# A spectral filter and a maxout MLP on one core: x of six batches loaded as bf16 for a dense first transform, in place of fp32 loads that are folded for a half-size one

## The chip, the cores and the metric

The kernel runs on 1 core of one Trainium2 chip. The metric is the device time of that core in microseconds (us), for one execution of the whole program. Lower is better.

## The reference

The reference is a real Fourier transform along the sequence, a product with a filter, the inverse transform, and then a small MLP with a maxout in the middle, on every token:

```
x: (8, 3072, 256) fp32;  filt_r, filt_i: (1537, 256);  w1, w2: (256, 1024);  w_out: (1024, 256)
X = rfft(x, axis=1);  Y = X * (filt_r + 1j * filt_i);  y = irfft(Y, n=3072, axis=1)
h1 = y @ w1;  h2 = y @ w2;  g = maximum(h1, h2);  out = g @ w_out        # (24576, 256) fp32
```

## The kernel before, in words

All of it is matmuls on TensorE (PE). The sequence of 3072 is split into 128 x 24. For each of the 8 batches the stages are:

- **f1**: the transform over the 128, as a matmul with the table C1. x stands in SBUF with 128 sequence rows as partitions and `n`, one of 24, beside the 256 features. The result is written to DRAM (tile `ad`) and read back in another order (`bt`, by `f1_read`).
- **f2** (`gen_f2`): eight steps `g` per batch. Each makes the transform over the 24 (`px`, matmuls with the table U, in quadrants of PE), multiplies by the filter on VectorE (`pq`, two instructions of 120x1024), and makes the inverse transform over the 24 (`pz`, matmuls with VP and VQ), evacuates it on ScalarE (`zt`) and writes it to DRAM (`zd`). A step's `pz` part is issued one step after its `px` part. `z_read` reads the result back (`zr`).
- **s4**: the inverse transform over the 128 (`py`, with G1), for one of 6 token blocks of a batch (512 tokens each).
- **moe_h** and **moe_o**: the MLP for one token block `tt`, in 8 steps `j`. The maximum is made as relu(y (w1 - w2)) and an additive term y (w2 w_out). `moe_h` (line 595) makes one of 8 hidden tiles, with a relu on ScalarE (line 600) or, for some, on VectorE (line 598). `moe_o` (lines 615 and 620) makes the output tiles of the block before; every fourth step VectorE copies a half block into `ot` (line 622), and at `j == 7` GpSimd's queue (POOL) stores `ot` to DRAM (line 627). There are two `ot` buffers.

The first batch goes through an opening of its own (`first_s1` to `first_t2`), with tables made by sines on ScalarE and small POOL and VectorE instructions. After about 47.7 us the main loop starts: `for tt in range(49)`, in it `for j in range(8)`; the step number is `8 * tt + j`. Each step issues `moe_h(tt, j)`, `moe_o(tt - 1, j)`, then whatever a hand-written plan has put on that step, and then, at `j` of 4 (or 6), the next `s4`. The plan (`plan_x`, `plan_f2`, `plan`) is what places the transform of the following batches between the MLP of the present one. The schedule is manual: every engine and every queue runs its instructions in the order of issue.

Three things matter for what follows.

First, how x of batches 2 to 7 is loaded. `load_p` (line 395) issues two DMAs on the SyncE queue (SP) for each of 6 groups `c` of four `n`. They bring fp32 rows p and p + 64 side by side into `xf`, with the two halves in opposite order in the upper 64 partitions. Five steps later `fold_x` (line 402) makes their sums and differences on GpSimd as bf16 (`xd`), with two instructions. These stand in the same in-order queue as the stores of `ot` at line 627.

Second, `f1_half` (line 410), called within six of the eight steps of `gen_f2(b)` for batch b + 1. With the sums and differences, the 128-row transform is two of 64 rows each. It takes four 64x64 quadrant matmuls with 512 columns per group, into two PSUM buffers `pa`, two ScalarE evacuations (line 413), and one write of `ad`. The columns of C1 are permuted for that, even before odd, by two POOL copies in the opening (line 639).

Third, PSUM: `ps` is a ring of 6 buffers, which `ph`, `px`, `pa`, `pz` and `py` share in the order of issue; `po` has two of its own.

Batch 1's x is loaded as bf16 by POOL DMAs that cast (`load_x`, line 101) and goes through the dense `f1` (line 379 and after), with C1 as 128x128 weights.

`f1_read` (line 423) reads `ad` in 8 DMAs on SP: two halves, two blocks, and even and odd apart.

Of the kernel before, what the change touches and what calls it, by code (L numbers as in the profile page):

```python
# [8 lines left out]
FP32 = mybir.dt.float32  # L9
BF16 = mybir.dt.bfloat16  # L10
AF = mybir.ActivationFunctionType
OP = mybir.AluOpType

B = 8
N = 3072
D = 256
HID = 1024
N1 = 128
N2 = 24
# [6 lines left out]
QUADS = ((0, 0), (1, 1), (0, 1), (1, 0))  # L26
# [3 lines left out]
def kernel(  # L30
# [25 lines left out]
    nc = tc.nc  # L56
    V, S, G, TE = nc.vector, nc.scalar, nc.gpsimd, nc.tensor

    const = ctx.enter_context(tc.tile_pool(name="const", bufs=1))
    C1 = const.tile([128, 128], BF16)  # L60
# [8 lines left out]
    I128 = const.tile([128, 128], BF16)  # L69

    dram = ctx.enter_context(tc.tile_pool(name="dram", bufs=2, space=bass.MemoryType.DRAM))
    xpool = ctx.enter_context(tc.tile_pool(name="xpool", bufs=7))
    apool = ctx.enter_context(tc.tile_pool(name="apool", bufs=5))
    bpool = ctx.enter_context(tc.tile_pool(name="bpool", bufs=2))
    pqpool = ctx.enter_context(tc.tile_pool(name="pqpool", bufs=6))
    zpool = ctx.enter_context(tc.tile_pool(name="zpool", bufs=2))
    zrpool = ctx.enter_context(tc.tile_pool(name="zrpool", bufs=2))
    late = ctx.enter_context(tc.tile_pool(name="late", bufs=1))
    w2b = late.tile([128, 2, HID], BF16, tag="l1", name="w2b")
    w2T = late.tile([128, 8, D], BF16, tag="l2", name="w2T")  # L80
    setup = ExitStack()
    ps = None
    init = setup.enter_context(tc.tile_pool(name="init", bufs=1))
# [12 lines left out]
    xb = {}  # L96
# [107 lines left out]
    load_f(1)  # L204

    Ct = init.tile([128, 128], BF16)
    Cz = init.tile([128, 128], BF16)

    def table_c():
        V.memset(kc[:, :, 1, 0:1], 32.0)  # L210
        V.memset(kc[:, 1, 0, 0:1], 64.0)
        p128 = init.tile([128, 1], FP32)
        V.tensor_scalar(p128, pid, 1.0 / 128.0, None, OP.mult)
        uc = init.tile([128, 2, 2, T], FP32)
        rc = init.tile([128, 2, 2, T], FP32)
        V.tensor_scalar(uc[:, 0], kc[:, 0], p128, 0.25, OP.mult, OP.add)
        V.tensor_scalar(uc[:, 1], kc[:, 1], p128, 0.5, OP.mult, OP.add)
        V.tensor_scalar(uc[:, 1, 0, 0:1], kc[:, 1, 0, 0:1], p128, 0.25, OP.mult, OP.add)
        V.tensor_scalar(rc, uc, RND, RND, OP.add, OP.subtract)
        V.tensor_tensor(uc, uc, rc, OP.subtract)  # L220
        for a in range(2):
            for b in range(2):
                S.activation(Ct.rearrange("p (b a h c u) -> p a b c h u", b=2, a=2, h=4, c=2)[:, a, b],
                             uc[:, a, b].rearrange("p (c h u) -> p c h u", c=2, h=4), AF.Sin, bias=zero, scale=TWO_PI)
        Cv = Cz.rearrange("p (h c u b a) -> p a b c h u", h=4, c=2, b=2, a=2)
        for a in range(2):
            for b in range(2):
                S.activation(Cv[:, a, b], uc[:, a, b].rearrange("p (c h u) -> p c h u", c=2, h=4),
                             AF.Sin, bias=zero, scale=TWO_PI)
# [86 lines left out]

    def table_g():
        pg = p2.tile([128, 128], BF16, tag="px", name="pg", bufs=4)
        TE.transpose(pg, Cz, I128)
        S.activation(G1, pg, AF.Copy)  # L320

    def tables_q(h, E):
# [42 lines left out]
    bt = {}  # L365
    zr = {}

    ad = {}
# [12 lines left out]
        if c % 2 == 1:  # L381
            nc.sync.dma_start(out=ad[b][:, 2 * c - 2:2 * c + 2], in_=at)

    big = {}

    def load_p(b, c):
        if c == 0:
            big[b] = late.tile([128, 3, 2, 2 * D], FP32, tag="l0", name="xf")
        if c < 3:
            xb[b, c] = big[b][:, c]  # L390
        else:
            xb[b, c] = late.tile([128, 2, 2 * D], FP32, tag="l%d" % (c - 2), name="xf")
        for m in range(2):
            o = x.offset + (b * N + 4 * c + 2 * m + 64 * N2 * m) * D
            nc.sync.dma_start(out=xb[b, c][64 * m:64 * m + 64],
                              in_=bass.AP(x.tensor, o, [[N2 * D, 64], [(1 - 2 * m) * 64 * N2 * D, 2], [1, 2 * D]]))

    def fold_x(b, c):
        xf = xb[b, c]
        xb[b, c] = xpool.tile([128, 2, 2 * D], BF16, tag="xb", name="xd")  # L400
        for i, op in enumerate((OP.add, OP.subtract)):
            G.tensor_tensor(xb[b, c][:, i], xf[:, 0], xf[:, 1], op)  # L402

    def f1_half(b, c):
        if c == 0:
            ad[b] = dram.tile([128, N2, D], BF16, tag="ad", name="ad")
        at = apool.tile([128, 4, D], BF16, tag="at", name="at")
        pa = [ps.tile([128, 2, D], FP32, tag="ps", name="pa") for _ in range(2)]
        for m, i in QUADS:
            TE.matmul(pa[m][64 * i:64 * i + 64], C1[64 * m:64 * m + 64, 64 * i:64 * i + 64],  # L410
                      xb[b, c][64 * m:64 * m + 64, i], start=True, stop=True)
        for m in range(2):
            S.activation(at[:, 2 * m:2 * m + 2], pa[m], AF.Copy)  # L413
        nc.sync.dma_start(out=ad[b][:, 4 * c:4 * c + 4], in_=at)

    def f1_read(b):
        bt[b] = bpool.tile([128, T, D], BF16, tag="bt", name="bt")
        src = ad[b].rearrange("(e t b a) n d -> b (a n) e t d", e=2, b=2, a=2)
        for h in (1, 0):
            for blk in range(2):  # L420
                for e in range(2):
                    t0 = 16 * e + 8 * h
                    nc.sync.dma_start(out=bt[b][64 * blk:64 * blk + 48, t0:t0 + 8], in_=src[blk][:, e, 8 * h:8 * h + 8])  # L423


    def z_read(b, h):
# [5 lines left out]
    def gen_f2(b):  # L432
# [25 lines left out]
                zt = None  # L458

        made = []  # L460
        for j, g in enumerate((4, 5, 6, 7, 2, 3, 1, 0)):
            px = [ps.tile([128, 2, D], FP32, tag="ps", name="px") for _ in range(2)]
            for i in range(2):
                for k, c in QUADS:
                    t_ = 16 * i + 4 * (g // 2) + 2 * c + g % 2
                    TE.matmul(px[k][64 * c:64 * c + 64, i], U[64 * k:64 * k + 48, 4 * g + 2 * i + c],  # L466
                              bt_[64 * k:64 * k + 48, t_], start=True, stop=True)
            pq = []
            for k in range(2):
                pq.append(pqpool.tile([128, 2, 2, D], BF16, tag="pq", name="pq"))  # L470
                V.tensor_tensor(pq[k][0:FROWS],  # L471
                                px[k][0:FROWS].rearrange("p (o i) d -> p o i d", o=1).to_broadcast([FROWS, 2, 2, D]),
                                F[0:FROWS, :, k, 2 * g:2 * g + 2], OP.mult)
            if b + 1 < B and j in (0, 1, 3, 4, 6, 7):
                f1_half(b + 1, (0, 1, 3, 4, 6, 7).index(j))
            pend.append((g, pq))
            if len(pend) > 1:
                s3(*pend.pop(0))
            yield
# [153 lines left out]
    def drain(g):  # L633
        for _ in g:
            pass

    table_c()
    for e in range(2):
        G.tensor_copy(C1.rearrange("p (e x u w) -> p e x u w", e=2, x=8, u=2)[:, e],
                      Cz.rearrange("p (x u e w) -> p e x u w", x=8, u=2, e=2)[:, e])  # L640
    Zt = late.tile([128, 2, 128, N2], BF16, tag="l0", name="Zt")
    At = init.tile([128, 4, 64, T], BF16, name="At")
    zeros(At[:, :, 48:64].rearrange("p h m t -> p h (m t)"), [4, 512])
    zeros(U.rearrange("p t (q x) -> p (t q) x", q=2)[:, :, 24:32], [64, 8])
# [66 lines left out]
    ps = ctx.enter_context(tc.tile_pool(name="ps", bufs=6, space=bass.MemoryType.PSUM))  # L711
# [10 lines left out]
    def plan(step, fn, *a):  # L722
        todo.setdefault(step, []).append((fn, a))

    def plan_x(n, steps):
        for c, s_ in enumerate(steps):
            plan(s_, load_p, n, c)
            plan(s_ + 5, fold_x, n, c)

    def plan_f2(n, steps, z1, z0):  # L730
        g = []

        def go():
            if not g:
                g.append(gen_f2(n))
            next(g[0], None)

        for s_ in steps:
            plan(s_, go)
        plan(z1, z_read, n, 1)  # L740
        plan(z0, z_read, n, 0)

    def spaced(first, gap, count):
        return [first + int(gap * i) for i in range(count)]
# [4 lines left out]
        plan(int(0.6 * (c - 1)), f1, 1, c, (S, V)[c % 2])  # L749
    plan(6, f1_read, 1)  # L750
    plan_f2(1, spaced(17, 1.9, 9), 28, 34)
    plan_x(2, (5, 7, 8, 10, 11, 13))
    plan(36, f1_read, 2)
    plan_x(3, spaced(32, 3.5, 6))
    plan_f2(2, spaced(60, 2.5, 9), 74, 81)
    plan(83, f1_read, 3)
    plan_x(4, spaced(76, 3.5, 6))
    plan_f2(3, spaced(104, 3, 9), 121, 129)
    plan(130, f1_read, 4)
    plan_x(5, spaced(122, 3.5, 6))  # L760
    plan_f2(4, spaced(150, 3.3, 9), 168, 178)
    plan(179, f1_read, 5)
    for n in range(5, B):
        o = 48 * (n - 5)
        if n + 1 < B:
            plan_x(n + 1, spaced(168 + o, 3.5, 6))
            plan(227 + o, f1_read, n + 1)
        plan_f2(n, spaced(197 + o, 3.4, 9), 216 + o, 226 + o)

    def in_f2(step):  # L770
# [2 lines left out]
    for tt in range(6 * B + 1):  # L773
        b, i = divmod(tt, 6)
# [40 lines left out]
```

## Time and profile before

| what | value |
|---|---|
| median of 2 runs | 582.9 us (581.5 and 584.31) |
| the profiled execution: its own time | 581.5 us |
| its span, first to last instruction | 579.7 us |
| mean granted TensorE clock | 0.962 |
| ScalarE relus of line 600 | 308 of 602 ns, 181.6 us |
| main MLP matmuls, line 620 | 1536 of 128x256, 234.5 us |
| folds on GpSimd, line 402 | 72 of 1264 ns, 89.3 us |
| fp32 loads of x on SP, line 395 | 72 of 256 KB |
| bf16 loads of x on POOL, line 101 | 12, 10.1 us from issue to landing in the median |
| stores of `ot` on POOL, line 627 | 47 of 512 KB, 4.4 us to landing in the median |
| SP's queue: packets' share of 16 DMA engines over the span | 49.6% |
| POOL's queue: the same | 17.9% |

How to read the profile: engines are PE (TensorE matmul), PEld (TensorE weight load, which overlaps PE), DVE (VectorE), ACT (ScalarE), POOL (GpSimd) and SP (SyncE, which only issues DMAs here). A line of the slices cuts the span into 40 equal parts, a digit giving tenths of it busy; PEclk is the granted clock, in tenths of full speed. A line of waits names the engine, the group that waited and its line in the kernel, then after `<-` what released it, then microseconds in total, times, and the longest. A line of the timeline gives start, duration, engine, line, operation, tiles and shapes, with the idle time before it and its releaser in brackets. A line of windows gives the window, its length, busy microseconds (and instructions) of PE, PEld, DVE, ACT and POOL, the granted clock, the DMA engines' busy share, and GB/s.

### The profile page before, as it was taken

To read this page: it belongs to the slowest core of one execution; us is meant where nothing else is said; L and a number is where in the kernel's file an instruction comes from. 1 tells how busy PE (TensorE), PEld (TensorE's weight loads), DVE (VectorE), ACT (ScalarE), POOL (GpSimd) and SP (SyncE) were. 2 spreads that over 40 slices of the span, in tenths; PEclk is the share of its full clock that TensorE was granted. 3 is DMA by queue.
4 is the path that set the end of the run, shared out by engine and by line. 5 is a ranking of instruction groups with operands and counts; after the bars stand their busy time and mean duration, and the time that the engine had idled before them with its cause. 6 is when DMAs were issued, how large, how long until landed. Compare 5 with 4: busy or idle time off the path is not lost.

```text
span 579.7 us, 12530 instructions
## 1 busy us (share of the span) xinstructions
PE 520.9 (90%) x5206; PEld 352.9 (61%) x5284; DVE 322.5 (56%) x437; ACT 337.2 (58%) x597; POOL 147.9 (26%) x168
## 2 busy tenths in 40 slices
PE   8898859995999969995999996999789999999997
PEld 3556536663566646673566763676456766677775
DVE  8887437431773446542775346745377368734442
ACT  7777538643686546853566563755456556655452
POOL 6681163126004070232405240051400000000000
PEclk9999979998799989998999997999979999999999
DMA  8982995898368954989449983789535873451102
GB/s 150 275 142 87 166 259 154 233 197 198 137 177 226 211 177 128 265 164 209 142 137 286 204 176 122 202 234 210 173 101 156 166 171 93 119 155 73 72 39 109
DMA packets 74093, 97.03 MB, mean 167 GB/s; under 512 B 5106, under 2 KB 49780, under 8 KB 73044
## 3 DMA queue, kind: packets, MB, share of 16 engines
q1 hardware_dynamic: 63012, 63.72, 49.6%
q0 software_dynamic: 11024, 32.51, 17.9%
q8 instruction: 41, 0.67, 0.5%
q14 instruction: 16, 0.13, 0.1%
HBM read 54.79 MB, written 47.19 MB: 176 GB/s over the span
## 4 chain that ended last, share of the span: by engine, by line
PE 62%; DMA 18%; ACT 5%; DVE 5%; SPq 4%; issue 3%; POOL 2%; POOLq 0%; DVEq 0%; ACTq 0%
PE po L620 22%; PE ph L595 20%; DMA xf<-in_x_dram 6%; DMA out_dram<-ot 5%; PE po L615 5%; SPq L423 3%; PE pz L447 3%; ACT at L413 3%; PE px L466 3%; DMA zd<-zt 2%; PE py L579 2%; POOL xd L402 2%; DVE pq L471 2%; DMA bt<-ad 2%; PE pa L410 2%
## 5 line engine op out<-in xcount | busy, mean ns | idle before, releaser
L600 ACT ACTIVATE gt<-ph 128x512 bf16<-128x512 f32 x308 | 181.6, 602 | 131.9 <-PE ph L595 131.3
L620 PE MATMUL po<-Wo,gt 128*128 128x256 bf16 x1536 | 234.5, 277 | 4.0 <-issue 0.7
L620 PEld LDWEIGHTS <-gt 128*128 128x128 bf16 x1536 | 152.6, 99 | 61.1 <-issue 3.3
L622 DVE COPY ot<-po 128x512 f32<-128x512 f32 x96 | 66.3, 690 | 156.2 <-PE po L620 106.2
L471 DVE TENSOR_TENSOR pq<-px,F 120x1024 bf16<-120x1024 f32 x112 | 131.7, 1219 | 30.6 <-PE px L466 29.7
L402 POOL TENSOR_TENSOR xd<-xf 128x512 bf16<-128x512 f32 x72 | 89.3, 1264 | 141.9 <-DMA xf<-in_x_dram 102.3
L627 POOL DMA_DIRECT2D out_dram<-ot x47 | 25.7, 548 | 271.8 <-DVE ot L622 271.8
L595 PEld LDWEIGHTS <-Wd 128*128 128x128 bf16 x768 | 71.5, 99 | 28.5 <-issue 19.8
L451 ACT ACTIVATE zt<-pz 112x512 bf16<-112x512 f32 x112 | 60.9, 600 | 26.1 <-PE pz L447 24.9
L413 ACT ACTIVATE at<-pa 128x512 bf16<-128x512 f32 x72 | 39.1, 595 | 57.8 <-PE pa L410 57.8
L598 DVE TENSOR_SCALAR gt<-ph 128x512 bf16<-128x512 f32 x76 | 52.2, 687 | 34.6 <-PE ph L595 23.8
L410 PE MATMUL pa<-xd,C 64*64 64x512 bf16 x144 | 17.5, 405 | 28.1 <-DVE pq L471 15.2
L447 PE MATMUL pz<-pq,VP 56*64 56x256 bf16 x448 | 31.7, 283 | 7.0 <-DVE pq L471 4.9
L579 PE MATMUL py<-G,zr 128*128 128x128 bf16 x384 | 29.9, 219 | 1.8 <-ACT at L413 1.0
L447 PE MATMUL pz<-pq,VQ 56*64 56x256 bf16 x448 | 30.7, 281 | 0.0
L579 PEld LDWEIGHTS <-zr 128*128 128x128 bf16 x384 | 25.3, 98 | 5.1 <-issue 3.3
L466 PE MATMUL px<-bt,U 48*64 48x256 bf16 x448 | 24.2, 281 | 1.0 <-DMA bt<-ad 1.0
L410 PEld LDWEIGHTS <-C 64*64 64x64 bf16 x144 | 5.0, 109 | 30.6 <-DVE pq L471 16.6
L447 PEld LDWEIGHTS <-VP 56*64 56x64 bf16 x448 | 15.6, 109 | 11.6 <-issue 6.8
L466 PEld LDWEIGHTS <-U 48*64 48x64 bf16 x448 | 8.6, 104 | 13.5 <-issue 13.2
L447 PEld LDWEIGHTS <-VQ 56*64 56x64 bf16 x448 | 14.7, 111 | 1.8
L529 DVE TENSOR_TENSOR pq<-px,F 120x1024 bf16<-120x1024 f32 x11 | 13.2, 1220 | 2.4 <-issue 1.1
(388 smaller groups left out, 604.6 us busy)
## 6 DMA issues: line engine op xcount, KB each, us to landing
out_dram<-ot POOLq DMA_DIRECT2D x47, 512.0 KB, 4.4
xf<-in_x_dram SPq DMA_DIRECT2D x72, 256.0 KB
ad<-at SPq DMA_DIRECT2D x42, 256.0 KB
bt<-ad SPq DMA_DIRECT2D x56, 192.0 KB
zd<-zt SPq DMA_DIRECT2D x56, 192.0 KB
zr<-zd SPq DMA_DIRECT2D x14, 768.0 KB
xb<-in_x_dram POOLq DMA_DIRECT2D x12, 256.0 KB, 10.1
wf<-in_moe_w_dram POOLq DMA_DIRECT2D x2, 1024.0 KB, 10.3
```

The costliest lines, as they stand in the source:

```text
L402: G.tensor_tensor(xb[b, c][:, i], xf[:, 0], xf[:, 1], op)
L413: S.activation(at[:, 2 * m:2 * m + 2], pa[m], AF.Copy)
L447: TE.matmul(pz[c][64 * k:64 * k + 64, i], W[64 * c:64 * c + 56, 2 * g + i, k], pq[k][64 * c:64 * c + 56, ri, i], start=(ri == 0), stop=(ri ...
L451: S.activation(zt[0:ROWS, c, o:o + 2], pz[c][0:ROWS], AF.Copy)
L466: TE.matmul(px[k][64 * c:64 * c + 64, i], U[64 * k:64 * k + 48, 4 * g + 2 * i + c], bt_[64 * k:64 * k + 48, t_], start=True, stop=True)
L471: V.tensor_tensor(pq[k][0:FROWS], px[k][0:FROWS].rearrange("p (o i) d -> p o i d", o=1).to_broadcast([FROWS, 2, 2, D]), F[0:FROWS, :, k, 2 ...
L579: TE.matmul(py[:, n], zr[b][:, 4 * i + n, 128 * dc:128 * dc + 128], G1, start=True, stop=True)
L595: TE.matmul(ph, Wd[:, dc, 128 * j:128 * j + 128], y_[:, dc].rearrange("p a b -> p (a b)"), start=(dc == 0), stop=(dc == 1))
L598: V.tensor_scalar(gt[tt][:, j], ph, 0.0, None, OP.max)
L600: S.activation(gt[tt][:, j], ph, AF.Relu)
L620: TE.matmul(p_, g_[:, jj, 128 * n:128 * n + 128], Wo[:, jj], start=False, stop=(jj == 7))
L622: V.tensor_copy(ot[tt][:, n - 1:n + 1], po[tt])
```

## The change

`load_p`, `fold_x` and `f1_half` go. x of batches 2 to 7 is loaded by `load_x` as bf16 with a cast on POOL's queue, 6 DMAs per batch, as batch 1's is. The dense `f1` then runs for all of these batches, one 128x512 matmul and one ScalarE evacuation for two of the 24 `n`, each on a plan step of its own and not within `gen_f2`. `C1` is written by the sines at once, in the order that was `Cz`'s, without the two copies. `f1_read` reads `ad` with 4 DMAs of twice the size. `xpool` has 8 buffers in place of 7, and the tiles in `late` no longer share memory with `xf`. The order of `t_` in `gen_f2` follows the new order of `ad`. The plan is another: loads 4 steps apart, 12 calls of `f1` 1 to 1.9 steps apart after them, `f1_read` one or two steps after the last, and `gen_f2` where it was, but for batch 4, which moves by one step. The opening is otherwise the same.

```diff
-    xpool = ctx.enter_context(tc.tile_pool(name="xpool", bufs=7))
+    xpool = ctx.enter_context(tc.tile_pool(name="xpool", bufs=8))
...
-        Cv = Cz.rearrange("p (h c u b a) -> p a b c h u", h=4, c=2, b=2, a=2)
+        Cv = C1.rearrange("p (h c u b a) -> p a b c h u", h=4, c=2, b=2, a=2)
...
-    def load_p(b, c):
...
-        for m in range(2):
-            o = x.offset + (b * N + 4 * c + 2 * m + 64 * N2 * m) * D
-            nc.sync.dma_start(out=xb[b, c][64 * m:64 * m + 64],
-                              in_=bass.AP(x.tensor, o, [[N2 * D, 64], [(1 - 2 * m) * 64 * N2 * D, 2], [1, 2 * D]]))
-
-    def fold_x(b, c):
-        xf = xb[b, c]
-        xb[b, c] = xpool.tile([128, 2, 2 * D], BF16, tag="xb", name="xd")
-        for i, op in enumerate((OP.add, OP.subtract)):
-            G.tensor_tensor(xb[b, c][:, i], xf[:, 0], xf[:, 1], op)
-
-    def f1_half(b, c):
...
-        pa = [ps.tile([128, 2, D], FP32, tag="ps", name="pa") for _ in range(2)]
-        for m, i in QUADS:
-            TE.matmul(pa[m][64 * i:64 * i + 64], C1[64 * m:64 * m + 64, 64 * i:64 * i + 64],
-                      xb[b, c][64 * m:64 * m + 64, i], start=True, stop=True)
-        for m in range(2):
-            S.activation(at[:, 2 * m:2 * m + 2], pa[m], AF.Copy)
-        nc.sync.dma_start(out=ad[b][:, 4 * c:4 * c + 4], in_=at)
-
     def f1_read(b):
         bt[b] = bpool.tile([128, T, D], BF16, tag="bt", name="bt")
-        src = ad[b].rearrange("(e t b a) n d -> b (a n) e t d", e=2, b=2, a=2)
+        src = ad[b].rearrange("(t b a) n d -> b (a n) t d", b=2, a=2)
         for h in (1, 0):
             for blk in range(2):
-                for e in range(2):
-                    t0 = 16 * e + 8 * h
-                    nc.sync.dma_start(out=bt[b][64 * blk:64 * blk + 48, t0:t0 + 8], in_=src[blk][:, e, 8 * h:8 * h + 8])
+                nc.sync.dma_start(out=bt[b][64 * blk:64 * blk + 48, 16 * h:16 * h + 16],
+                                  in_=src[blk][:, 16 * h:16 * h + 16])
...
-            if b + 1 < B and j in (0, 1, 3, 4, 6, 7):
-                f1_half(b + 1, (0, 1, 3, 4, 6, 7).index(j))
...
     def plan_x(n, steps):
         for c, s_ in enumerate(steps):
-            plan(s_, load_p, n, c)
-            plan(s_ + 5, fold_x, n, c)
+            plan(s_, load_x, n, c)
+
+    def plan_f1(n, steps, read):
+        for c, s_ in enumerate(steps):
+            plan(s_, f1, n, c)
+        plan(read, f1_read, n)
...
-    plan_x(2, (5, 7, 8, 10, 11, 13))
-    plan(36, f1_read, 2)
-    plan_x(3, spaced(32, 3.5, 6))
+    plan_x(2, spaced(8, 4, 6))
+    plan_f1(2, spaced(34, 1, 12), 46)
     plan_f2(2, spaced(60, 2.5, 9), 74, 81)
-    plan(83, f1_read, 3)
-    plan_x(4, spaced(76, 3.5, 6))
+    plan_x(3, spaced(44, 4, 6))
+    plan_f1(3, spaced(70, 1.5, 12), 88)
     plan_f2(3, spaced(104, 3, 9), 121, 129)
-    plan(130, f1_read, 4)
-    plan_x(5, spaced(122, 3.5, 6))
-    plan_f2(4, spaced(150, 3.3, 9), 168, 178)
-    plan(179, f1_read, 5)
+    plan_x(4, spaced(90, 4, 6))
+    plan_f1(4, spaced(112, 1.8, 12), 132)
+    plan_f2(4, spaced(151, 3.3, 9), 169, 179)
     for n in range(5, B):
         o = 48 * (n - 5)
-        if n + 1 < B:
-            plan_x(n + 1, spaced(168 + o, 3.5, 6))
-            plan(227 + o, f1_read, n + 1)
+        plan_x(n, spaced(138 + o, 4, 6))
+        plan_f1(n, spaced(158 + o, 1.9, 12), 180 + o)
         plan_f2(n, spaced(197 + o, 3.4, 9), 216 + o, 226 + o)
```

More of the change, by code (lines that the diff above doesn't have):

```diff
@@ L78 @@
     late = ctx.enter_context(tc.tile_pool(name="late", bufs=1))
-    w2b = late.tile([128, 2, HID], BF16, tag="l1", name="w2b")
-    w2T = late.tile([128, 8, D], BF16, tag="l2", name="w2T")
+    w2b = late.tile([128, 2, HID], BF16)
+    w2T = late.tile([128, 8, D], BF16)
     setup = ExitStack()
@@ L206 @@
     Ct = init.tile([128, 128], BF16)
-    Cz = init.tile([128, 128], BF16)
     def table_c():
@@ L318, in table_g @@
         pg = p2.tile([128, 128], BF16, tag="px", name="pg", bufs=4)
-        TE.transpose(pg, Cz, I128)
+        TE.transpose(pg, C1, I128)
         S.activation(G1, pg, AF.Copy)
@@ L382, in f1 @@
             nc.sync.dma_start(out=ad[b][:, 2 * c - 2:2 * c + 2], in_=at)
-    big = {}
-    def load_p(b, c):
[L387 to L392, printed above, removed]
-        for m in range(2):
-            o = x.offset + (b * N + 4 * c + 2 * m + 64 * N2 * m) * D
-            nc.sync.dma_start(out=xb[b, c][64 * m:64 * m + 64],
-                              in_=bass.AP(x.tensor, o, [[N2 * D, 64], [(1 - 2 * m) * 64 * N2 * D, 2], [1, 2 * D]]))
-    def fold_x(b, c):
-        xf = xb[b, c]
-        xb[b, c] = xpool.tile([128, 2, 2 * D], BF16, tag="xb", name="xd")
-        for i, op in enumerate((OP.add, OP.subtract)):
-            G.tensor_tensor(xb[b, c][:, i], xf[:, 0], xf[:, 1], op)
-    def f1_half(b, c):
-        if c == 0:
-            ad[b] = dram.tile([128, N2, D], BF16, tag="ad", name="ad")
-        at = apool.tile([128, 4, D], BF16, tag="at", name="at")
-        pa = [ps.tile([128, 2, D], FP32, tag="ps", name="pa") for _ in range(2)]
-        for m, i in QUADS:
-            TE.matmul(pa[m][64 * i:64 * i + 64], C1[64 * m:64 * m + 64, 64 * i:64 * i + 64],
-                      xb[b, c][64 * m:64 * m + 64, i], start=True, stop=True)
-        for m in range(2):
-            S.activation(at[:, 2 * m:2 * m + 2], pa[m], AF.Copy)
-        nc.sync.dma_start(out=ad[b][:, 4 * c:4 * c + 4], in_=at)
     def f1_read(b):
         bt[b] = bpool.tile([128, T, D], BF16, tag="bt", name="bt")
-        src = ad[b].rearrange("(e t b a) n d -> b (a n) e t d", e=2, b=2, a=2)
+        src = ad[b].rearrange("(t b a) n d -> b (a n) t d", b=2, a=2)
         for h in (1, 0):
             for blk in range(2):
-                for e in range(2):
-                    t0 = 16 * e + 8 * h
-                    nc.sync.dma_start(out=bt[b][64 * blk:64 * blk + 48, t0:t0 + 8], in_=src[blk][:, e, 8 * h:8 * h + 8])
+                nc.sync.dma_start(out=bt[b][64 * blk:64 * blk + 48, 16 * h:16 * h + 16],
+                                  in_=src[blk][:, 16 * h:16 * h + 16])
     def z_read(b, h):
@@ L460, in gen_f2 @@
         made = []
-        for j, g in enumerate((4, 5, 6, 7, 2, 3, 1, 0)):
+        for g in (4, 5, 6, 7, 2, 3, 1, 0):
             px = [ps.tile([128, 2, D], FP32, tag="ps", name="px") for _ in range(2)]
@@ L464, in gen_f2 @@
                 for k, c in QUADS:
-                    t_ = 16 * i + 4 * (g // 2) + 2 * c + g % 2
+                    t_ = 8 * (g // 2) + 4 * c + 2 * (g % 2) + i
                     TE.matmul(px[k][64 * c:64 * c + 64, i], U[64 * k:64 * k + 48, 4 * g + 2 * i + c],
@@ L637 @@
     table_c()
[L638 to L641, printed above, removed]
+    Zt = late.tile([128, 2, 128, N2], BF16, name="Zt")
     At = init.tile([128, 4, 64, T], BF16, name="At")
```

## The prediction

> **What bounds the kernel now.** I read the busy table and the slices first, then the waits, then one stall in order of time, then the same stretch of work batch by batch.
>
> ```profile
> PE 520.9 (90%) x5206; PEld 352.9 (61%) x5284; DVE 322.5 (56%) x437; ACT 337.2 (58%) x597; POOL 147.9 (26%) x168
> PE   8898859995999969995999996999789999999997
> PEclk9999979998799989998999997999979999999999
> ```
>
> TensorE (PE) is the bound at 90%, and no other engine is near. Seven slices fall below 9 after the opening, and near each the granted clock falls too. The waits say who holds PE there:
>
> ```profile
> POOL out_dram L627 <- DVE ot L622: 271.8, 33, 14.1
> POOL xd L402 <- DMA xf<-in_x_dram: 102.3, 12, 17.4
> DVE ot L622 <- DMA out_dram<-ot: 49.7, 6, 11.1
> PE pa L410 <- DVE pq L471: 15.2, 5, 6.4
> PE pa L410 <- POOL xd L402: 7.0, 2, 6.4
> PE pa L410 <- DVE y__4127 L584: 5.9, 1, 5.9
> PE pz L447 <- DVE pq L471: 4.9, 2, 4.2
> ```
>
> PE's last four rows are 33.0 us in ten waits. The third row has six waits of some 8 us, one to a batch, and the second is long enough to be behind them. In order of time, one of the six, from the timeline of DVE and that of all engines (start, duration, engine, line; the wait before it in brackets):
>
> ```profile
> 120.45 0.69 DVE L622 COPY ot<-po 128x512 f32<-128x512 f32 x1 [1.81 <-PE po L620]
> 125.42 6.82 SPq L395 DMA_DIRECT2D xf<-in_x_dram  x6
> 134.11 2.50 POOL L402 TENSOR_TENSOR xd<-xf 128x512 bf16<-128x512 f32 x2 [10.44 <-DMA xf<-in_x_dram]
> 136.56 0.56 POOL L627 DMA_DIRECT2D out_dram<-ot  x1
> 143.29 0.69 DVE L622 COPY ot<-po 128x512 f32<-128x512 f32 x1 [11.09 <-DMA out_dram<-ot]
> 145.17 0.64 PE L410 MATMUL pa<-xd,C 64*64 64x512 bf16 x3 [6.35 <-DVE pq L471]
> ```
>
> The copy at 120.45 completes a block of output, which could be stored at 121.1. POOL, in order, is held by folds whose fp32 x is not there (its loads sit on SP behind the reads of bt), so the store leaves at 136.56, 15.4 us late. It frees its buffer at 143.2; DVE waits 11.1 us in its ot copy, the products pq queue behind that copy, and PE behind them. By batch (length, busy us of PE, PEld, DVE, ACT, POOL, clock, DMA share):
>
> ```profile
> 120.25:190.05 69.80, 60.57 (x586) 40.83 (x593) 34.42 (x40) 40.86 (x76) 20.52 (x20) 0.93 0.78 186
> 190.05:257.73 67.68, 60.95 (x593) 41.51 (x601) 34.00 (x39) 41.92 (x78) 17.51 (x17) 0.95 0.77 191
> 257.73:327.01 69.28, 61.04 (x592) 41.54 (x600) 38.38 (x46) 38.46 (x71) 21.05 (x21) 0.95 0.77 190
> 327.01:395.14 68.13, 61.77 (x592) 41.80 (x600) 38.29 (x46) 38.68 (x71) 18.58 (x19) 0.95 0.77 189
> 395.14:463.49 68.35, 61.69 (x592) 41.73 (x600) 38.30 (x46) 38.66 (x71) 10.25 (x12) 0.95 0.67 159
> 463.49:520.91 57.42, 56.56 (x568) 39.43 (x576) 38.27 (x46) 32.82 (x59) 3.20 (x6) 1.00 0.53 136
> ```
>
> The windows run from one batch's first s4 to the next one's. The last has all of gen_f2 but no f1_half, no fold and no x load: 57.4 us against a mean of 68.65, at full clock. The 11.2 us between them are f1_half, the stall and what follows from it.
>
> **The change, part by part.** *Folds and fp32 loads go.* 72 folds of 1.26 us (91 us of POOL) and 72 issues of some 0.6 us on SP (43 us) leave. POOL then holds no instruction that waits for a late transfer ahead of a store, so the six stalls should go: 33.0 us of PE's waits. The clock comes back with them: the five rows at 0.93 to 0.95, and 0.95 in the 72.5 us window ahead of them, make 22 us of lost clock; some of that lies inside the stalls themselves. I bound the work lost between 11 and 22 us and take 16, the middle.
>
> *Dense f1 in place of quadrants.* In the timeline four quadrant matmuls (L410 x4) start at 238.92 and L447 follows at 239.14: 0.22 us for four n. Two 128x512 matmuls (L595 x2) start at 241.95 and L615 follows at 242.38: 0.43 us. So PE pays 0.21 us more for each of 36, 7.6 us, all on the path. It cannot be below 0 or over 36 x 0.43 = 15.5.
>
> *Evacuation.* 72 copies of 0.595 us on ACT either way, now one to a step in place of two to an f2 step. ACT has 33 to 42 us of work in a 57 us batch, so they are hidden; from step 70 to 82, where all relus are on ACT, its 0.60 + 1.20/2.5 + 0.60/1.5 + 0.6/8 = 1.56 us a step stand just under PE's 1.034 + 0.97/2.5 + 0.25/1.5 = 1.59 (an f2 step is the last batch's 57.4 less 49.6, by 8). In return px, px, pz, pz no longer shares the six PSUM buffers with two pa: "PE ph waits for ACT at L413" (5.3 us in 21 waits) may go; 0 to 5.3, within the second sum below.
>
> *x by the POOL queue, cast to bf16.* 36 issues at 0.56 us (row L101, 537 to 589 ns) are 20 us of POOL. Each is planned 20 steps, some 25 us, ahead of its matmul, and landed in 7.5 to 15.4 us (median 10.1) in the opening, the nearest row. All earlier users of its xpool buffer are done steps before, so no load holds POOL's queue. Hidden while landing stays under 25 us. A store has about 12 steps, 14 us, before its buffer is wanted; stores landed in 2.9 to 10.8 us (median 4.4). Hidden.
>
> The Trainium skill's page "SBUF", section "SBUF: two separate sides", speaks against this: descriptors of a DMA issued by GpSimd can be locked out while VectorE is in a two-port mode, and a transfer of 620 ns became one of 3100. The stores here are such DMAs beside a VectorE that is 56% busy, and their issue took 534 to 627 ns in all 47, so I see no lock here. By the page, as an estimate, 36 loads would each be some 2.5 us later, 91 us if none of it were hidden (some 623 us); by the rows the sum below stands.
>
> *bt read in four DMAs for eight.* Same bytes. For batches 6 and 7 the read is planned one step later than before (step 228 for 227, needed at 245 as before), for batch 2 at 46 and needed at 60. The chain shows its landing and that of the ad write ahead of it:
>
> ```profile
> 58.57 3.95 DMA ad<-at
> 389.53 12.04 DMA bt<-ad
> ```
>
> Seventeen steps are at least 17.6 us at the 1.034 us of a bare step (8.27 us per eight in the last batch), enough for 16; batch 2's 14 steps, with f1(2) just ended, are about as long as the 16. I take 0, and up to 4 us a batch as the other end.
>
> *Opening.* Two POOL copies (0.41 us at 13.4) go, and a wait for one x buffer: hidden, since C1 is first used after 48 us. 0, at most 1 us either way.
>
> **The sum** against the profiled span of 579.7 us. First way: 33.0 + 16 - 7.6 = 41.4 off, 538.3. Second way: five batches become 57.42 + 12 x 0.25 = 60.4 each, 41.1 off; the batch ahead of them loses 8.2 us of waits and 2.2 of clock and pays 1.3, 9.1 off: 529.5. The second also counts the DVE backlog after each stall, but its model batch had a lighter DMA load (0.53). I take 532 between them, nearer the second. The profiled execution took 581.5 us, 1.8 over its span, and the median of the two runs is 582.9, so I forecast 534 us.
>
> **Rivals.** *A new, smaller wait takes over: bt late.* If bt is 2 us late in each of six batches, 12 us come back: 546. If 4 us late, long enough to drop the clock as the 3.5 us wait at 348.65 did, 6 x (4 + 2.6) = 40: 572. For it: batch 2's thin lead and a DMA share of 0.78 that goes to about 0.8 in a shorter batch. Against it: now px waits 1.0 us in all for bt, and SP loses 72 issues.
>
> *The change doesn't do what it says.* If the store is late through crowded DMA engines and not through POOL's queue, the six stalls stay and dense f1 is added: 579.7 + 7.6 + 1.8 = 589, no change. For it: the store that left at 116.73 held the ot copy until 126.80, ten us, while bt was read. Against it: that one cost PE nothing; those that did had left up to 15 us late.
>
> *Slower: stores behind loads.* Loads and stores now share the software queue all through. If a store behind loads takes the place of the fold, some 18 stores (three to a batch, over the 20 steps of loads) are exposed. Each us over 14 costs 18 us; it eats the 48 us of gain at a mean landing of some 17 us, and at 18 us, 18 x 4 = 72 less 48 is 24 more than before: 607. Against it: 10.8 us was the worst of 47, and x's packets fall in number with bf16.
>
> **How the numbers follow.** Forecast (520 to 548) 0.62; bt late (548 to 572) 0.18; no change (572 to 594) 0.11; slower (over 594) 0.09. Two per cent, about what a measurement of this kernel can tell, is 571 to 594. So faster 0.80, same 0.11, slower 0.09. The range 520 to 570 leaves out the last two cases; the likeliest case's own is 520 to 548.
>
> **What would show it.** Right: no PE wait over 3 us after the opening, clock 1.00 in every window from 62 us on, batches of 60 to 61 us, "DVE ot waits for out_dram" near nothing, two dense matmuls some 0.43 us apart from their follower, POOL busy near 75 us. Wrong: PE px waiting for bt (first rival); ot still waiting, its store having left on time (second); store landings over 14 us or f1 waiting for xb (third). If dense f1 or ACT cost more than I say, the batches are clean but over 62 us.

## The result, and the profile after

The changed kernel takes 531.4 us in the median of two runs (531.24 to 531.57), against 582.9 before: a ratio of 0.9116, 95% interval 0.9021 to 0.9212. The forecast was 534, with a range of 520 to 570. The profiled execution has a span of 529.8 us at a mean clock of 0.999.

The busy table and the slices of the page:

```profile
PE 509.7 (96%) x5133; PEld 347.5 (66%) x5212; DVE 321.9 (61%) x437; ACT 336.2 (63%) x597; POOL 77.7 (15%) x130
PE   9898999999999999999999999999999999999994
PEclk9999999999999999999999999999999999999999
```

PE is busy at 96%; the low slices between the opening and the last one are gone, and so are the drops of the clock. Of the waits after, those that bear on the argument:

```profile
POOL out_dram L591 <- DVE ot L586: 409.5, 46, 12.1
DVE ot L586 <- PE po L584: 109.6, 74, 4.5
DVE pq L437 <- PE px L432: 27.5, 34, 1.7
PE ph L559 <- DVE pq L437: 2.3, 7, 0.3
PE pz L413 <- DVE pq L437: 0.8, 1, 0.8
```

Stores now wait only for the copy that fills `ot`, and that copy only for PE. "DVE ot waits for out_dram", 49.7 us before, has no line left; PE's longest wait for DVE in the main loop is 0.8 us. Batch by batch, with the same columns as before:

```profile
47.72:110.90 63.18, 60.80 (x591) 41.04 (x600) 38.60 (x47) 45.00 (x83) 4.82 (x9) 1.00 0.78 184
110.90:170.32 59.42, 58.39 (x574) 39.94 (x581) 34.42 (x40) 40.51 (x76) 6.96 (x13) 1.00 0.77 191
230.33:290.34 60.01, 59.10 (x579) 40.60 (x588) 38.27 (x46) 38.15 (x71) 6.43 (x12) 1.00 0.76 178
410.66:468.07 57.41, 56.55 (x568) 39.45 (x576) 38.27 (x46) 32.82 (x59) 3.20 (x6) 1.00 0.53 131
468.07:529.80 61.73, 54.74 (x426) 40.06 (x430) 22.36 (x33) 25.95 (x44) 3.74 (x7) 0.99 0.18 69
```

The first window is 9.4 us shorter than before. The five batches after it are 59.4 to 60.3 us each (two are shown) and together 43.5 us shorter. The batch without any f1 is unchanged. The last stretch is 2.9 us longer, with the same work in it: something at the end has grown. 9.4 + 43.5 - 2.9 is the 50 us of the two spans.

### The profile page after: what moved, and what is told of

Its sections match the earlier page's. It is cut to its first block, busy times and chain, and to the rows that moved or that the text cites. A ratio compares the mean times of both kernels' runs of the same rounds, so it can differ in the third digit from the quotient of the medians.

```text
span 529.8 us, 12177 instructions
## 1 busy us (share of the span) xinstructions
PE 509.7 (96%) x5133; PEld 347.5 (66%) x5212; DVE 321.9 (61%) x437; ACT 336.2 (63%) x597; POOL 77.7 (15%) x130
## 4 chain that ended last, share of the span: by engine, by line
PE 76%; DVE 1%; issue 1%
PE po L584 30%; PE ph L559 26%; PE po L579 7%; PE pz L413 4%; PE px L432 3%; PE py L543 3%; PE pa L378 3%; DVE pq L437 1%; DVE ot L586 0%
## 5 line engine op out<-in xcount | busy, mean ns | idle before, releaser
L584 PE MATMUL po<-Wo,gt 128*128 128x256 bf16 x1536 | 229.8, 273 | 3.0
L584 PEld LDWEIGHTS <-gt 128*128 128x128 bf16 x1536 | 150.3, 98 | 57.5
L559 PEld LDWEIGHTS <-Wd 128*128 128x128 bf16 x768 | 70.0, 98 | 27.8 <-issue 12.5
L477 ACT ACTIVATE at<-pa 128x512 bf16<-128x512 f32 x78 | 46.9, 601 | 12.3 <-PE pa L378 10.8
L378 PE MATMUL pa<-xb,C 128*128 128x512 bf16 x83 | 31.1, 381 | 0.1
L413 PE MATMUL pz<-pq,VP 56*64 56x256 bf16 x448 | 28.5, 271 | 0.8 <-DVE pq L437 0.8
L413 PE MATMUL pz<-pq,VQ 56*64 56x256 bf16 x448 | 27.9, 268 | 0.0
L101 POOL DMA_DIRECT2D xb<-in_x_dram x48 | 26.1, 550 | 1.8 <-DMA Fs<-in_filt_i_dram 1.5
L413 PEld LDWEIGHTS <-VP 56*64 56x64 bf16 x448 | 13.1, 106 | 2.7 <-issue 1.5
L477 ACT ACTIVATE F<-pf 128x1024 bf16<-128x1024 f32 x10 | 10.2, 1031 | 6.5 <-PE pf L134 6.5
```

The costliest lines, as they stand in the source:

```text
L378: TE.matmul(pa, C1, xb[b, c // 2][:, 2 * (c % 2):2 * (c % 2) + 2], start=True, stop=True)
L413: TE.matmul(pz[c][64 * k:64 * k + 64, i], W[64 * c:64 * c + 56, 2 * g + i, k], pq[k][64 * c:64 * c + 56, ri, i], start=(ri == 0), stop=(ri ...
L477: S.activation(out_, in_, AF.Copy)
L559: TE.matmul(ph, Wd[:, dc, 128 * j:128 * j + 128], y_[:, dc].rearrange("p a b -> p (a b)"), start=(dc == 0), stop=(dc == 1))
L584: TE.matmul(p_, g_[:, jj, 128 * n:128 * n + 128], Wo[:, jj], start=False, stop=(jj == 7))
```

## The experiments

Theory A is the prediction's: a fold that waits in POOL's queue for a late x holds the stores behind it, then DVE, then PE, and the clock drops after each stall. Against it stood crowded DMA engines (B), the quadrant stage inside f2 steps (C), and POOL's work as such (D). Ratios are to the kernel before on the same chip, with 95% intervals.

**The kernel before, folds later.**

```diff
-            plan(s_ + 5, fold_x, n, c)
+            plan(s_ + (5 if n == 2 else 17), fold_x, n, c)
```

> The kernel before, with the folds of batches 3 to 7 planned 17 steps after their loads in place of 5; nothing else changes, so all 72 folds, all fp32 loads and the quadrant matmuls stay. Theory A (the cost is POOL's queue: a fold that waits for a late x holds the stores behind it, then DVE's ot copy, pq and PE): five of six stalls go, five batches become about 57.4 + 1.8 = 59.2 us, the first keeps its 72.5; span about 532, time about 534. Theory B (crowded DMA engines or SP's load make stores and bt late, whenever the fold runs): within 2% of the kernel before, 572 to 594. Theory C (the quadrant step inside an f2 step is what stalls): also 572 to 594.

Measured: 539.7 us, ratio 0.9294 (0.9254 to 0.9335). The first windows of this kernel:

```profile
47.73:122.11 74.38, 64.70 (x612) 42.91 (x612) 38.77 (x47) 44.60 (x83) 17.07 (x16) 0.91 0.77 193
122.11:182.08 59.97, 58.01 (x595) 39.85 (x593) 34.59 (x40) 40.62 (x76) 20.64 (x20) 1.00 0.85 208
182.08:242.04 59.96, 58.67 (x603) 40.50 (x600) 33.98 (x39) 41.89 (x78) 20.52 (x20) 1.00 0.87 218
```

The five batches fall from 343.2 to 300.1 us, with all folds, fp32 bytes and quadrants still there and the DMA share up from 0.77 to 0.87. Their PE is without work for 7.4 us (length less PE busy) where it was 37.2, so 29.8 of the 43.1 us are idle time. The other 13.3 lie in time that PE counts as busy; the clock, at 0.93 to 0.95 before and 1.00 now, is what changed there. B and C fall for these five batches, which are 0.8 us longer than I said. The first window keeps its stall, since batch 2's folds were left where they were: PE waits there for the fold's own output (`pa` for `xd`, 7.1 us in two waits), and no store is part of it. That window is also 1.9 us longer than in the kernel before; the granted clock stood at half for 3.4 us from 47.7 us on in this run, ahead of any stall.

**The kernel before, stores on another queue.**

```diff
-                G.dma_start(out=dst[:, 4 * i:4 * i + 4], in_=ot[tt])
+                S.dma_start(out=dst[:, 4 * i:4 * i + 4], in_=ot[tt])
```

> The kernel before, with its 47 stores of ot issued on ScalarE's queue in place of POOL's; folds stay where they were. Theory A: stores leave as soon as their copy is done, the ot copies no longer wait, and the stalls that came through DVE go (26 of 33 us of PE's waits and most of the lost clock), those that waited for xd itself (7.0 us) stay; ScalarE pays for 47 issues of some 0.6 us, beside its 58% load; time 535 to 550. Theory B (crowded DMA engines): stores land no sooner, 572 to 594.

Measured: 548.75 us, 0.9456 (0.9402 to 0.9511). The five batches are 60.6 to 61.8 us. The folds wait for x longer than ever (178.2 us in 15 waits), and in these batches that no longer stalls PE, since no store is behind them. The first window is 75.5 us and keeps its stall, as the expectation said of the waits for `xd` itself:

```profile
PE pa L410 <- POOL xd L402: 9.3, 2, 8.6
```

ScalarE pays for the stores, as expected: its relus wait 41.0 us in total for DVE's `ot` copies, which the store ahead of them waits for.

**The changed kernel with POOL's work put back**, 72 additions of the folds' size on data that is always there, two to a load:

```diff
             plan(s_, load_x, n, c)
+            plan(s_ + 5, busy_pool)
```

> The changed kernel with 72 GpSimd additions of the folds' size (128x512, fp32 in, bf16 out, about 1.26 us each) put back on POOL's queue, two of them five steps after each load of x, on data that is always there. Theory A: it is the fold's wait for x and not its work that costs; the time stays at 531 to 533. Theory D (POOL's work itself, as queue occupancy or by the port it shares with DVE): some or all of 91 us of POOL work shows, 540 or more.

Measured: 532.3 us, 0.9169 (0.9123 to 0.9215), with the five batches of the changed kernel to 0.03 us. D falls: work of this size on POOL is free. (The additions took 1.04 us each, a little less than the folds' 1.26.)

**The changed kernel with POOL's queue held**, four times, by 16 or by 28 such additions in a row:

```diff
+    for t in (14, 20, 26, 32):
+        plan(8 * t, hold_pool)
```

> The changed kernel, with POOL's queue held four times, in the f2 windows of batches 3 to 6, by 16 GpSimd additions of 1.26 us on data that is always there, 20.2 us right behind one store. The next store is ready some 10.5 us later and so leaves 9.7 us late; with some 5 us to land it still beats its buffer's next use, 12 steps or about 15.6 us after it was ready. Theory A: no stall, 531 to 533. Theory D (POOL's work costs in itself): part of 81 us, over 540.

> The same with 28 additions, 35.3 us: the next store leaves 24.8 us late. Theory A: 24.8 + 5 to land less 15.6 leaves DVE some 14 us in its ot copy and PE some 10 us without work, after which the clock drops: four stalls of 10 + 2.6 us, 570 to 590, though no fold, no fp32 load and no quadrant stage is in the kernel. Theory B (crowded DMA engines made the stalls) and theory C (the quadrant stage did): no stall without them, 531 to 540.

Measured: 532.5 us with 16 (0.916, 0.9103 to 0.9217) and 571.6 us with 28 (0.9844, 0.979 to 0.9898). From one start to the next the additions took 1.11 us, so the holds were 17.8 and 31.2 us and not the 20.2 and 35.3 of the expectations. Of the 28, the first hold, from the timelines of POOL and DVE and, for its fifth row, of all engines:

```profile
192.69 31.20 POOL L694 TENSOR_TENSOR w2T<-w1z 128x512 bf16<-128x512 f32 x28
201.80 0.69 DVE L586 COPY ot<-po 128x512 f32<-128x512 f32 x1 [1.67 <-PE po L584]
223.84 1.11 POOL L591 DMA_DIRECT2D out_dram<-ot  x2
229.00 0.69 DVE L586 COPY ot<-po 128x512 f32<-128x512 f32 x1 [14.50 <-DMA out_dram<-ot]
230.34 0.58 PE L559 MATMUL ph<-y__3818,Wd 128*128 128x512 bf16 x1 [6.78 <-DVE y__3818 L548]
```

It is the stall of the kernel before, made without a fold: the store is ready at 202.5, leaves 21.4 us late, DVE waits 14.5 us in its copy, PE 6.8. With 16 the store at 212.91 was 8 us late (ready at 204.95), the other three were 6 to 7 us late, and nothing waited for any of the four. In that run DVE did wait 3.4 us once for a store, and PE not at all, but that store left 0.3 us after it was ready (at 286.85) and took 12.7 us to land, while `bt` was read. That fits crowded DMA engines (B), but it stalled nothing. So 8 us of lateness cost nothing and some 20 us (19.5 to 21.4 in the four holds of 28) stalled PE each time.

**The changed kernel with one small wait**, a GpSimd copy of 48x8 elements that needs bt:

```diff
         plan(read, f1_read, n)
+        plan(read + 1, hold_pool, n)
```

> The changed kernel, with one small GpSimd copy (48x8) that reads bt put on POOL's queue a step after each f1_read, so that the queue is held once a batch until the last-issued part of bt has landed, up to some 16 us. A store that falls into it leaves up to 12 us late. Theory A with the slack of a_hold16's expectation (about 10 us of lateness before anything waits): 531 to 536; theory A with no slack: seven stalls, over 560.

Measured: 568.4 us, 0.9784 (0.9719 to 0.985): as a number that is the second case, "over 560", which stood for stores without slack. The run with 16 additions shows slack, so that is not the reason: I had the size of the hold wrong. Six such copies of 0.19 us wait 127.7 us, the longest 26.4, where I had expected up to 16. One of them:

```profile
246.16 0.19 POOL L691 COPY w2T<-bt 48x8 bf16<-48x8 bf16 x1 [25.50 <-DMA bt<-ad]
246.69 0.53 POOL L591 DMA_DIRECT2D out_dram<-ot  x1 [0.34 <-issue]
249.77 0.69 DVE L586 COPY ot<-po 128x512 f32<-128x512 f32 x1 [10.62 <-DMA out_dram<-ot]
```

POOL runs ahead of the other engines, so it stands at the copy from 220 on, long before the read of bt is issued at 234.57. The store behind was ready at 229.4 and left 17.3 us late. Behind five of the six copies the first store was 9.9 to 18.2 us late, and DVE waited 5.3 to 12.0 us; behind the other it was 6.6 us late, and nothing waited. About 1 us of POOL's work costs 37 us.

**Quadrants and dense, by themselves.** The changed kernel with four quadrant matmuls per group, and with each dense matmul twice:

```diff
+                for m, i in QUADS:
+                    TE.matmul(p2_[b][m][64 * i:64 * i + 64], C1[64 * m:64 * m + 64, 64 * i:64 * i + 64],
+                              xb[b, c // 2][64 * m:64 * m + 64, 2 * i:2 * i + 2], start=True, stop=True)
...
+        for _ in range(2 if b > 1 else 1):
             TE.matmul(pa, C1, xb[b, c // 2][:, 2 * (c % 2):2 * (c % 2) + 2], start=True, stop=True)
```

> The changed kernel, with four 64x64 quadrant matmuls in place of two dense 128x512 ones for batches 2 to 7, on x that is not folded, so the sums and differences are left out and the output is not the reference's; its time is that of the matmuls alone. If the dense stage costs 0.21 us more for each of 36 groups and all of it is on the path, 7.6 us go: time about 524. If the dense matmuls are hidden, or the quadrants have a price of their own outside f2 steps, 530 to 532.

> The changed kernel, with every dense f1 matmul of batches 2 to 7 issued twice into the same PSUM buffer, the second overwriting the first with the same result. If the dense stage's price is 0.215 us for each 128x512 matmul and all on the path, 72 more cost 15.5 us: 547, and each batch goes from 60.0 to 62.6 us. If some of it hides in waits of PE, less.

Measured: 535.7 us with quadrants (0.9229, 0.9189 to 0.9269), slower than the changed kernel and not 7.6 us faster; 546.9 us with double dense matmuls (0.9424, 0.9372 to 0.9477), as expected: four of its five batches are 62.6 us, one of them here, 2.59 more for 12 matmuls.

```profile
175.61:238.21 62.60, 62.27 (x603) 41.79 (x601) 34.00 (x39) 41.94 (x78) 6.44 (x12) 1.00 0.76 176
```

So the dense price was right, 0.216 us each, and the quadrants' was wrong: 535.7 is above both numbers of that expectation. Between full matmuls, on the timeline of the quadrant run:

```profile
192.69 0.49 PE L594 MATMUL po<-Wo,gt 128*128 128x256 bf16 x3
193.11 0.41 PE L384 MATMUL pa<-xb,C 64*64 64x512 bf16 x4
193.46 0.60 PE L569 MATMUL ph<-y__3242,Wd 128*128 128x512 bf16 x2
```

Three 256-column matmuls are 0.32 us at 0.107 each, so they end their issue at 193.01 and the quadrants begin 0.10 us after that; the full matmul that follows begins 0.35 us later, not 0.22. A group costs 0.45 us from 193.01 to 193.46, about what two dense matmuls do (0.43). PE's weight loads at that line of ph waited 25.8 us for "issue", against 12.5 in the changed kernel, and ph waited 5.6 us for pq, against 2.3, with two `pa` buffers taken at once.

**The kernel before, mended**: all folds 17 steps after their loads, batch 2 by bf16 loads and dense f1.

```diff
-            plan(s_ + 5, fold_x, n, c)
+            plan(s_ + 17, fold_x, n, c)
...
-            if b + 1 < B and j in (0, 1, 3, 4, 6, 7):
+            if 2 < b + 1 < B and j in (0, 1, 3, 4, 6, 7):
```

> The kernel before, with all folds 17 steps after their loads and batch 2 loaded as bf16 and sent through the dense f1, as in the changed kernel; batches 3 to 7 keep fp32 loads, folds and quadrants. Theory A (POOL's queue order was the whole cost): no stall is left, 47.7 + 63.2 + 5 x 60.0 + 57.4 + 58.8 = 527 of span, 529 us, level with or below the changed kernel. Theory C (the half-size stage inside f2 steps is worse in itself): over 540.

Measured: 529.3 us, 0.9128 (0.9091 to 0.9164), as expected. Its first two windows:

```profile
47.62:110.67 63.05, 60.68 (x590) 40.93 (x600) 38.60 (x47) 44.96 (x83) 4.81 (x9) 1.00 0.81 194
110.67:170.64 59.97, 57.54 (x586) 39.87 (x593) 34.61 (x40) 40.61 (x76) 20.64 (x20) 1.00 0.88 216
```

The fold and the half-size stage were not at fault; where a fold stood in the queue was. Beyond batch 2, the new loads and the dense stage are not needed for the gain: with 60 of the 72 folds, and the quadrants of five batches, still there, this kernel is 2 us below the changed one. In the profiles that difference lies in the last stretch (59.3 us against 61.7), which the next runs explain.

**The end of the program.** The last three POOL stores on SP, loads of x merged in pairs, and the changed kernel again beside them:

```diff
-                G.dma_start(out=dst[:, 4 * i:4 * i + 4], in_=ot[tt])
+                (G if tt < 6 * B - 4 else nc.sync).dma_start(out=dst[:, 4 * i:4 * i + 4], in_=ot[tt])
...
-        G.dma_start(out=t_, in_=src[:, 4 * c:4 * c + 4, :])
+            G.dma_start(out=t_, in_=src[:, 4 * c:4 * c + 8, :])
```

> The changed kernel once more, unaltered, so that the three others can be set against it on one chip: 531.4 us, between 530.5 and 532.5.

> The changed kernel, with the last three of its 47 POOL stores issued on SP, whose queue is empty by then. In the changed kernel GpSimd's last drain takes 9.2 us from its last store's issue (6.3 in the kernel before) and ends 2.7 us after SP saw the last store land. If that drain is on the path to the end, it now starts some 25 us sooner, ends hidden, and the time falls by about 2.7 us, to 528.7. If the drain only waits for the end of something else, the time stays at 531.4.

> The changed kernel, with x of batches 2 to 7 loaded by 18 DMAs of twice the size in place of 36. GpSimd's last drain was 6.3 us with 69 DMAs on POOL's queue and 9.2 with 105. If it goes with the number of DMAs (0.08 us for each of the added ones), it is 7.7 us here and the time is 530; if with their bytes or descriptors, it stays at 9.2 us and the time at 531.4. Loads that land later than their matmul would show as PE waiting for xb.

Measured: 531.3 us for the changed kernel again (0.9164, 0.9127 to 0.9201), 528.5 us with the stores on SP (528.04 to 528.75; 0.9111, 0.9075 to 0.9146), 530.9 us with merged loads (0.9148, 0.9111 to 0.9185). With merged loads the last stretch is 1.5 us shorter in the profile, as the drain is, but the time fell by 0.4 us only, which is within the spread of the runs. The drain's line, by source, in the kernel before, the changed one, the merged one and the one with stores on SP (duration in ns, shortest, median, longest; then first and last start):

```profile
L810 POOLq DRAIN  x3: 46/102/6264, 572.7 to 579.4; - x3
```

```profile
L772 POOLq DRAIN  x3: 46/102/9204, 519.8 to 529.5; - x3
```

```profile
L776 POOLq DRAIN  x3: 46/93/7734, 519.6 to 527.8; - x3
```

```profile
L772 POOLq DRAIN  x3: 46/93/8959, 494.8 to 526.0; - x3
```

With 69, 105, 87 and 102 DMAs on POOL's queue that is one straight line, 0.63 us and 0.0817 us for each DMA, whether large or small; the mended kernel before, with 75, has 6.756 us, on the same line. In the kernel before it ended together with SP's wait for the last store; in the changed kernel 2.7 us after it. With three stores on SP it starts at 494.8 and is over long before the end. This version is the fastest of the study, below both kernels; its runs and those of the changed kernel (530.92 to 532.54) do not overlap.

## Why the prediction was right, step by step

**The stalls and their cause**: right for five of the six. Undoing either half of it, the fold's wait or the store's place behind it, removes those five from the kernel before; a wait alone puts stalls into the changed kernel. The first stall is another: the six waits of `ot` are not "one to a batch", as I read them. Two lie in the window from 120.25 on (126.80 and 143.29, the first of which cost PE nothing) and none in the window ahead of it, where PE stood 6.4 us (to 77.97) for the late fold's output itself. It goes with the fold, and so was rightly in the 33 us, but no store has a part in it.

**Their size**: right in sum. I took 33 us of PE's waits and 16 of clock. The experiment with later folds gives 29.8 and 13.3 for five of the six stalls; nothing was lost to a late bt (no line of PE px waiting for it), and the first rival did not come.

**Dense f1, 7.6 us more**: wrong. The failed step is "So PE pays 0.21 us more for each of 36". Its dense half holds (0.216 us a matmul). A quadrant group did not cost 0.22: in the kernel before without stalls, a batch with six of them is 59.97 us against 57.42 without, 0.42 each, next to nothing under the dense stage's 0.43. I read 0.22 where a group stood between other quadrant matmuls, and left out what comes after it: two `pa` with two `px` and two `pz` fill the ring of six, and "PE ph waits for ACT at" is 6.3 us in 25 waits in that kernel, 0.17 for each of 36 groups:

```profile
PE ph L595 <- ACT at L413: 6.3, 25, 0.3
```

I had that wait as a possible gain of "0 to 5.3", and did not set it against the quadrants' price. Where a full matmul follows at once, the turn adds 0.1 as well. The second sum had a slip of its own here: it priced a dense matmul at 0.25 us, not at the 0.215 of the first, and so each of its batches at 60.4 us; they came out at 59.4 to 60.3.

**The cast loads on POOL**: right. 48 loads landed in 4.2 to 15.8 us (median 8.2) and PE never waited for one in the main loop; stores landed in 2.9 to 10.5 us. The rival on the other side, stores behind loads, needed a landing of 17 us. The lock on descriptors that the page "SBUF" of the Trainium skill describes ("SBUF: two separate sides") does not show here: the 48 loads took 531 to 621 ns to issue and the 47 stores 534 to 544.

**The second rival**, crowded DMA engines: wrong, by the later folds, with which five batches run without a stall at a DMA share of up to 0.87.

**The end**: missed, 2.9 us on the path. I counted each moved DMA's issue, 0.56 us, and not what it adds to GpSimd's last drain. Without it the span would be 526.9: the first sum, 538.3, is 11 us over that and the second, 529.5, is 3. The drain and the dense term err in opposite ways, so it is in part luck that the forecast is nearer than its terms.

**Small slips**, none of which moves the forecast: two more slices after the opening are below 9 (58.0 to 72.5 us, and the last), with no fall of the clock; 36 x 2.5 is 90 and not 91; 534 and 40 are 574 and not 572; batch 2's loads are planned 26 to 16 steps ahead of their matmuls and not 20; the reads of batches 3, 4 and 5 were planned later too, by 5, 2 and 1 steps, and none was late.

## What to carry to other kernels

On an in-order queue that carries stores, look for every instruction that can wait for a transfer, and ask how late the store behind it may be; its own duration says nothing. Plan such an instruction when its data is surely there, or give the stores a queue of their own. A share of PE time saved by quadrants must be read between full matmuls and with the PSUM buffers it holds, not inside a run of quadrants.

## What the runs showed of the hardware

Where a store was the last instruction on its queue, GpSimd's drain at the end of the program took 0.63 us and 0.0817 us for each DMA that the queue had issued, over five counts (69, 75, 87, 102, 105); issuing the last few stores elsewhere hides it. With all stores on ScalarE's queue, 22 DMAs were left on GpSimd's and the drain began while folds were still running: it took 4.8 us, where the line gives 2.4, so the line is shown for the first case only.

A turn from full to quadrant matmuls, or back, cost PE about 0.1 us here (0.10 and 0.13 in the lines above).

With each of the six PE gaps of 3.5 to 6.4 us in the kernel before, the granted clock went to half, 2.2 to 4.6 us after the gap had begun, and stayed there for 6.8 us, once 10.2; it was back at full 4.5 to 7.3 us after the gap's end. The Trainium skill's page "TensorE: Matmul & The Clock Gate" (Part 1) has the half rate after an idle window of about 3.4 us, and about as long to warm up again: the half rate agrees, the way back was longer here, up to twice that. A gap is not needed, though: in the run with holds of 16 additions, and in that with later folds, the clock stood at half for 3.4 us from 47.7 us on, with no PE gap over 1.2 us ahead of it. In the first of them, which has no stall, the first window was 65.3 us against 63.2 in the changed kernel. Why it happened in these two runs only is open.
